# First layer of a two-layer network on 512 tokens at a time, behind a banded attention, on one core of Trainium2

## The chip, the core and the metric

The kernel runs on one core of one Trainium2 chip. Times are device microseconds (us) of an execution. The kernel before takes 738.41 us in the median of three runs (738.12 to 741.0).

## The reference, cut to what matters

```python
# q, k, v: batch 4, 8 heads, 768 positions, 64 per head; n_global = 8, n_local = 96
scores = q @ k.T / sqrt(64)
keep   = (key < n_global) | ((0 <= rel) & (rel < n_local))       # rel = query - key
scores = where(keep, scores - slope[head] * dist, -1e9)          # ALiBi distance
a      = softmax(scores)                                          # the sum gets 1e-9
x      = (a @ v) laid out as 3072 tokens x 512
h      = x @ w_in                                                 # 512 -> 2048
out    = (0.5 * h * (1 + erf(h / sqrt(2)))) @ w_out               # GELU, 2048 -> 512
```

w_in and w_out arrive as 64-bit numbers; all arithmetic is of 32-bit floats.

## The kernel before, in words

The 3072 tokens are cut into twelve **chunks** of 256 tokens, the 2048 hidden columns into eight **slices** of 256. A **step** t is one pair (chunk, slice) from the list `STEPS`; there are 96. The matmuls read their operands in a form that keeps fewer bits of a number, so every number that matters is split into a high part (ending in h) and a low part (ending in l), and each product is three matmuls: high times high, high times low, low times high.

In step t the first layer (`m1`, L463) fills one PSUM bank `h{t}`: two halves f of 128 hidden columns, for each of four pieces d of the 512 inputs three matmuls over 256 tokens. That is 24 matmuls of 128x256, each with its own 128x128 stationary weights (`winh`, `winl`), and the moving operand is x of the chunk (`xh`, `xl`). Then `gelu`: ScalarE (ACT) makes `gr` from `h` (L473), GpSimd (POOL) makes the high part `gh` (helper line L145), VectorE (DVE) the low part `gl` (helper line L151). The second layer (`m2`, L493) has `gh`/`gl` of 128 tokens as stationary operand, and 512 columns of `wouth`/`woutl` as moving operand: 12 matmuls of 128x512 that add into two accumulators `acc{c}_0`, `acc{c}_1`, one bank each, over all eight slices of the chunk. After the last slice ACT copies them out and a DMA stores them.

The attention of a chunk is spread over some ten steps, from `START[c]` on (`att`, the tables `EV` and `EVN` say at which step each part comes): k, q and v are loaded and split (POOL and DVE), scores `s` (PE, L338), masked on DVE (`n`, L343), the exponential on ACT (L358) in two batches of four heads, the division by the sum on POOL (`n<-n,su`, L371), transposes `t` (PE, L384), their copy in two parts `pt` (ACT L391, then DVE L151), `av` (PE, L426), and from that `t1`, `t3` (ACT, DVE) and the two parts of x. Every `s`, `t` and `av` takes a PSUM bank from its first matmul to the end of its last reader. Chunks 0 and 1 (`NATIVE`) use another form. While steps 0 to 8 run, the weights are still being loaded and split (`split_weights`, ACT and DVE), one slice after another; therefore chunks 0 and 1 go through slices 2 to 7 side by side, and chunks 2 to 11 one after another.

PSUM has eight banks. Two belong to the pool `ps_acc` (accumulators), six to the pool `ps` (`h`, `s`, `t`, `av`, and the accumulators of chunk 1).

The code is written step by step: `run` emits for each T the first layer of step T+1, the attention parts that fall on T, and the second layer of step T. The framework's scheduler then sets the order on each engine by priorities, its own estimate of times and the buffers that are free, and chooses the bank of each tile. Each engine works in its order; a matmul waits for what it reads, and the first one into a bank for the last reader of the bank's previous tile.

Of the kernel before, what the change touches and what calls it, by code (L numbers as in the profile page):

```python
# [68 lines left out]
class Fast:  # L69
    def __init__(self, tc, ctx, qT, kT, v, w, out, limits):  # L70
        self.tc, self.nc = tc, tc.nc
        self.qT, self.kT, self.v, self.w, self.out = qT, kT, v, w, out
# [322 lines left out]
    def av_mm(self, c, h):  # L395
        nc = self.nc
        p, hh = divmod(h, 2)
        pts = self.parts(c)
        first = c % CPB == 0
        pt = self.pt_t.pop((c, h))  # L400
        vt = self.vt.pop((c, h))
        if h == 0:
            self.x[c] = (self.xp.tile([P, NP, CT], F32R, name=f"xh{c}", tag="xh"),
                         self.xp.tile([P, NP, CT], F32R, name=f"xl{c}", tag="xl"))
        if c in NATIVE:
            if hh == 0:
                self.avp = self.bank([P, 2, 2, D], f"av{c}_{p}", [P, 2, 2, 2 * D])
            av = self.avp
            for i, (j, a) in enumerate(pts):
                vi = (a if first else 2 * j + a)  # L410
                js = [x for x in pts if x[0] == j]
                nc.tensor.matmul(av[:, hh, j, :], lhsT=pt[:, i, :], rhs=vt[:, vi, :],
                                 start=(j, a) == js[0], stop=(j, a) == js[-1])
            if hh == 1:
# [4 lines left out]
                self.xs[c, p] = xs
            return  # L420
        av = self.bank([P, 2, 2, P], f"av{c}_{h}")
        for i, (j, a) in enumerate(pts):
            vi = (a if first else 2 * j + a)
            js = [x for x in pts if x[0] == j]
            start, stop = (j, a) == js[0], (j, a) == js[-1]
            nc.tensor.matmul(av[:, j], lhsT=vt[:, vi], rhs=pt[:, i], start=start, stop=stop)  # L426
        if hh == 0:
            self.t3[c, p] = (self.sm.tile([P, 2, P], F32, name=f"t1_{c}_{p}", tag="t1", bufs=1),
                             self.sm.tile([P, 2, P], F32, name=f"t3_{c}_{p}", tag="t3", bufs=1))
        t1, t3 = self.t3[c, p]  # L430
# [4 lines left out]
        nc.vector.tensor_tensor(out=t3[hr], in0=av[hr, :, 0, :], in1=t1[hr], op=ALU.add)
        if hh == 1:
            xh, xl = self.x[c]
            t3f = t3.rearrange("p j q -> p (j q)")
# [10 lines left out]
        nc.scalar.copy(xh, xt)  # L449
        self.lo_dve(xl, xt, xh)  # L450

    def m1(self, t, f):
        nc = self.nc
        c, s = STEPS[t]
        xh, xl = self.x[c]
        wh, wl = self.win[s]
        if f == 0:
            self.h[t] = self.bank([P, 2, CT], f"h{t}")
        hp = self.h[t]
        n = 0  # L460
        for d in range(NP):
            for w, x in ((wh, xh), (wh, xl), (wl, xh)):
                nc.tensor.matmul(hp[:, f, :], lhsT=w[:, d, f * P:(f + 1) * P], rhs=x[:, d, :],  # L463
                                 start=n == 0, stop=n == 3 * NP - 1)
                n += 1

    def gelu(self, t):
        nc = self.nc
        hp = self.h.pop(t)
        gh = self.gp.tile([P, 2, CT], F32R, name=f"gh{t}", tag="gh")  # L470
        gl = self.gp.tile([P, 2, CT], F32R, name=f"gl{t}", tag="gl")
        gr = self.gp.tile([P, 2, CT], F32, name=f"gr{t}", tag="gr", bufs=1)
        self.table(nc.scalar.activation(out=gr, in_=hp, func=AF.Gelu))  # L473
# [4 lines left out]
    def m2(self, t, k):
        nc = self.nc
        c, s = STEPS[t]  # L480
        gh, gl = self.g[t]
        wh, wl = self.wout[s]
        if s == 0:
            if c == 1:
                self.acc[c, k] = self.bank([P, DM], f"acc{c}_{k}")
            else:
                self.acc[c, k] = self.ps_acc.tile([P, DM], F32, name=f"acc{c}_{k}", tag="ps_acc")
        acc = self.acc[c, k]
        ks = slice(k * P, (k + 1) * P)
        n = 0  # L490
        for f in range(2):
            for g, w in ((gh, wh), (gh, wl), (gl, wh)):
                nc.tensor.matmul(acc, lhsT=g[:, f, ks], rhs=w[:, f, :],  # L493
                                 start=s == 0 and n == 0, stop=s == NST - 1 and n == 5)
                n += 1
        if s == NST - 1:
# [284 lines left out]
```

## Time and profile before

| | |
|---|---|
| median of three runs | 738.41 us |
| the profiled execution: time, span of its profile | 739.55 us, 737.5 us |
| granted TensorE clock, mean | 0.998 |
| TensorE matmul busy (PE) | 715.7 us, 97% of the span |
| VectorE busy (DVE) | 504.1 us, 68% |
| ScalarE busy (ACT) | 355.2 us, 42 activation table loads among it |
| GpSimd busy (POOL) | 309.7 us, 42% |
| first-layer matmuls, 128x256 | 2304 |
| second-layer matmuls, 128x512 | 1152 |

Busy PE time is the time in which at least one matmul is in flight. A matmul's row is longer than the distance to the next one, since matmuls overlap: what one costs in a row of its kind is the distance from start to start, and that is read from the chain of the work that ended last, or from the timeline. "Idle before" is the time that an engine stood still ahead of an instruction, with what ended it.

### The profile page before, as it was taken

What the parts mean: (1) busy time and instruction counts of PE and PEld (TensorE: products, weight loads), DVE (VectorE), ACT (ScalarE), POOL (GpSimd) and SP (SyncE); (2) the same over time, 40 slices, a digit from 0 to 9 for tenths busy, and PEclk for the clock granted to TensorE, in tenths of its full rate; (3) what the DMA queues carried; (4) which work ended last, traced back from release to release, by engine and by line L of the source; (5) the groups of instructions that cost most, each with busy time, mean ns of one, the idle gap of its engine ahead of it and who ended that gap; (6) DMA issues with size and microseconds to landing.
All of it is one profiled execution on the core that took longest, in us unless ns stands there. A gap on an engine that the chain in (4) does not pass through costs nothing.

```text
span 737.5 us, 13431 instructions
## 1 busy us (share of the span) xinstructions
PE 715.7 (97%) x4617; PEld 647.1 (88%) x4617; DVE 504.1 (68%) x1317; ACT 355.2 (48%) x906; POOL 309.7 (42%) x572
## 2 busy tenths in 40 slices
PE   5999999898999999999999999999999999999996
PEld 3778999788999999999889999999899999989995
DVE  6998898956857867856757867857758767634210
ACT  4666656355355455355355355354455455452101
POOL 2311125665345555553544654643544654431110
PEclk9999999999999999999999999999999999999999
DMA  8986524225424434334335434234335331100000
GB/s 244 275 218 221 160 89 144 74 62 157 118 85 126 132 100 116 101 92 128 107 97 135 116 108 129 87 101 133 101 104 137 111 112 44 44 16 1 30 1 32
DMA packets 74395, 80.91 MB, mean 110 GB/s; under 512 B 12368, under 2 KB 63056, under 8 KB 74320
## 3 DMA queue, kind: packets, MB, share of 16 engines
q1 hardware_dynamic: 70144, 73.16, 34.9%
q10 hardware_dynamic: 4176, 6.82, 2.6%
q8 instruction: 38, 0.62, 0.3%
q14 instruction: 37, 0.30, 0.1%
HBM read 73.66 MB, written 6.29 MB: 108 GB/s over the span
## 4 chain that ended last, share of the span: by engine, by line
PE 71%; DVE 10%; DMA 7%; POOL 5%; ACT 4%; issue 3%; SPq 1%; ACTq 0%; DVEq 0%; POOLq 0%
PE acc L493 29%; PE h L463 29%; PE av L426 4%; PE s L338 4%; PE t L384 4%; POOL n L371 3%; DMA w<-w 3%; DMA vr<-v 2%; DMA c<-w 2%; ACT n L358 2%; DVE wb L188 1%; DVE wb L186 1%; DVE n L343 1%; POOL gh L145 1%; DVE wb L184 1%
## 5 line engine op out<-in xcount | busy, mean ns | idle before, releaser
L463 PE MATMUL h<-xh,winh 128*128 128x256 f32 x768 | 219.7, 286 | 0.0
L463 PE MATMUL h<-xl,winh 128*128 128x256 f32 x768 | 218.5, 285 | 0.0
L463 PE MATMUL h<-xh,winl 128*128 128x256 f32 x768 | 217.1, 283 | 0.0
L493 PE MATMUL acc<-wouth,gh 128*128 128x512 f32 x384 | 153.7, 400 | 3.3 <-POOL gh L145 3.3
L493 PE MATMUL acc<-woutl,gh 128*128 128x512 f32 x384 | 151.1, 394 | 0.0
L463 PEld LDWEIGHTS h<-xh,winh 128*128 128x128 f32 x768 | 146.7, 191 | 2.3
L463 PEld LDWEIGHTS h<-xl,winh 128*128 128x128 f32 x768 | 146.9, 191 | 2.0
L463 PEld LDWEIGHTS h<-xh,winl 128*128 128x128 f32 x768 | 146.8, 191 | 0.4
L493 PE MATMUL acc<-wouth,gl 128*128 128x512 f32 x384 | 142.7, 395 | 1.2 <-DVE gl L151 1.2
L151 DVE TENSOR_TENSOR gl<-gr,gh 128x512 fp32r<-128x512 f32 x96 | 68.7, 716 | 91.2 <-POOL gh L145 91.2
L473 ACT ACTIVATE gr<-h 128x512 f32<-128x512 f32 x96 | 57.5, 599 | 147.1 <-PE h L463 102.4
L371 POOL TENSOR_SCALAR n<-n,su 128x256 f32<-128x256 f32 (+1 forms) x160 | 78.4, 511 | 83.6 <-DVE su L363 73.8
L145 POOL TENSOR_SCALAR gh<-gr 128x512 fp32r<-128x512 f32 x96 | 66.0, 687 | 99.6 <-ACT gr L473 99.6
L145 POOL TENSOR_SCALAR vt<-vr 128x256 fp32r<-128x256 f32 (+1 forms) x80 | 34.5, 432 | 150.1 <-DMA vr<-v 74.8
L358 ACT ACTIVATE n<-n,mn 128x256 f32<-128x256 f32 (+1 forms) x192 | 91.8, 480 | 4.9 <-DVE mn L343 4.4
L493 PEld LDWEIGHTS acc<-wouth,gl 128*128 128x128 f32 x384 | 72.1, 188 | 18.0 <-DVE gl L151 3.2
L493 PEld LDWEIGHTS acc<-wouth,gh 128*128 128x128 f32 x384 | 72.4, 189 | 15.8 <-POOL gh L145 5.0
L493 PEld LDWEIGHTS acc<-woutl,gh 128*128 128x128 f32 x384 | 72.5, 189 | 12.3
L391 ACT CAST pt<-t 128x512 fp32r<-128x512 f32 (+1 forms) x80 | 44.4, 555 | 67.8 <-PE t L384 60.3
L433 ACT COPY t<-av 64x256 f32<-64x256 f32 x80 | 29.4, 368 | 96.1 <-PE av L426 93.6
L343 DVE CUSTOM_DVE_ANT_0 n<-s,pen 128x256 f32<-128x256 f32 (+1 forms) x192 | 68.6, 392 | 4.4 <-PE s L338 2.8
L384 PE MATMUL t<-ident,n 128*128 128x128 f32 x352 | 60.5, 294 | 1.3 <-ACT gr L473 0.6
(87 smaller groups left out, 1071.4 us busy)
## 6 DMA issues: line engine op xcount, KB each, us to landing
w<-w SPq DMA_DIRECT2D x32, 512.0 KB, 4.1
c<-w SPq DMA_DIRECT2D x32, 512.0 KB, 3.8
kr<-kT SPq DMA_DIRECT2D x112, 112.0 KB, 2.7
qr<-qT SPq DMA_DIRECT2D x84, 128.0 KB, 2.9
vr<-v SPq DMA_DIRECT2D x48, 128.0 KB, 2.4
out<-o ACTq DMA_DIRECT2D x24, 256.0 KB, 2.2
kr<-kT SPq DMA_DIRECT2D x28, 128.0 KB, 2.7
vr<-v SPq DMA_DIRECT2D x32, 96.0 KB, 2.2
```

The costliest lines, as they stand in the source:

```text
L145: self.nc.gpsimd.tensor_scalar(out=out, in0=in_, scalar1=scale, scalar2=0.0, op0=ALU.mult, op1=ALU.add)
L151: self.nc.vector.tensor_tensor(out=out, in0=in_, in1=hi.bitcast(F32), op=ALU.subtract)
L338: nc.tensor.matmul(sp[:, j, :w], lhsT=qq[:, hh, j * P:(j + 1) * P], rhs=kt[:, t, 0 if first else j, :w], start=t == 0, stop=t == 1)
L343: nc.vector.tensor_tensor_reduce(out=nn[:, j, :w], in0=sp[:, j, :w], in1=pen, scale=-slope(h), scalar=3e38, op0=ALU.add, op1=ALU.min, accu ...
L358: ins = nc.scalar.activation(out=nn[:, j, :w], in_=nn[:, j, :w], func=AF.Exp, bias=mn[:, i:i + 1], scale=-1.0, accum_out=su[:, i:i + 1])
L371: nc.gpsimd.tensor_scalar(out=nn[:, j, :w], in0=nn[:, j, :w], scalar1=su[:, i:i + 1], scalar2=0.0, op0=ALU.mult, op1=ALU.add)
L384: nc.tensor.transpose(tp[:, i, :], nn[:, j, a * P:(a + 1) * P], self.ident)
L391: nc.scalar.copy(pt[:, :, 0, :], tp[:, :n, :])
L426: nc.tensor.matmul(av[:, j], lhsT=vt[:, vi], rhs=pt[:, i], start=start, stop=stop)
L463: nc.tensor.matmul(hp[:, f, :], lhsT=w[:, d, f * P:(f + 1) * P], rhs=x[:, d, :], start=n == 0, stop=n == 3 * NP - 1)
L473: self.table(nc.scalar.activation(out=gr, in_=hp, func=AF.Gelu))
L493: nc.tensor.matmul(acc, lhsT=g[:, f, ks], rhs=w[:, f, :], start=s == 0 and n == 0, stop=s == NST - 1 and n == 5)
```

## The change

Four things change together.

- **Pairs.** From slice 2 on chunks 0 and 1 share each step, chunks 2 and 3 stay alone, and from chunk 4 on the chunks rotate: chunk 4 does slices 0 to 3 alone (steps 32 to 35), then chunks 4 and 5 share slices 4 to 7 (steps 36 to 43), chunks 5 and 6 slices 0 to 3 (steps 44 to 51), chunks 6 and 7 slices 4 to 7, and so on; chunk 11 does its last four slices alone (steps 92 to 95). A shared step is one half f of a slice for two chunks: `m1` has 12 matmuls of 128x512 in place of 24 of 128x256, with 12 weight loads in place of 24. There are 68 shared steps and 28 others, 96 as before. `m2` keeps 12 matmuls of 128x512 in each step; in a shared step they go into four accumulators, three into each.
- **The ring.** x of three chunks lies in one tile for each part (`xall`), chunk c at place c mod 3, so that two chunks can be one moving operand: two runs of 256 tokens, side by side or with the third place between them.
- **One pool.** The eight banks are one pool. In the rotation four of them hold accumulators all the time, so four are left for `h`, `s`, `t` and `av`, where six were.
- **The attention's starts.** Chunk 4 starts its attention at step 18 (before 19), chunk 5 at 24 (27), chunks 6 to 11 four steps earlier than before; the first matmul of chunk c is now in step 8c - 4 (chunk 5 on), before in step 8c.

```diff
-START = [-10, -6, 4] + [8 * c - 13 for c in range(3, NCH)]
-
-STEPS = [(0, 0), (0, 1), (1, 0), (1, 1)] + [(c, s) for s in range(2, NST) for c in range(2)]
-STEPS += [(c, s) for c in range(2, NCH) for s in range(NST)]
+START = [-10, -6, 4, 11, 18, 24] + [8 * c - 17 for c in range(6, NCH)]
+STEPS += [((0, 1), s, f) for s in range(2, NST) for f in range(2)]
...
-        self.xp = pool("xp", 3)
+        self.xp = pool("xp")
...
-        self.ps_acc = pool("ps_acc", 2, space=PSUM)
-        self.ps = pool("ps", 6, space=PSUM)
+        self.ps = pool("ps", 8, space=PSUM)
+        self.xall = tuple(self.xp.tile([P, NP, 3, CT], F32R, name=n) for n in ("xh", "xl"))
...
+    def tokens(self, x, cs, d):
+        i = sorted(c % 3 for c in cs)
+        return x[:, d, i[0], :] if len(i) == 1 else x[:, d, i[0]:i[1] + 1:i[1] - i[0], :]
...
+        if len(cs) == 1:
+            out, f, ds = self.h[t][:, half * CT:(half + 1) * CT], half, range(NP)
+        else:
+            out, ds = self.h[t].rearrange("p (k q) -> p k q", k=2), range(2 * half, 2 * half + 2)
+        for d in ds:
+            for n, (w, x) in enumerate(((wh, xh), (wh, xl), (wl, xh))):
+                nc.tensor.matmul(out, lhsT=w[:, d, f * P:(f + 1) * P], rhs=self.tokens(x, cs, d),
+                                 start=d == 0 and n == 0, stop=d == NP - 1 and n == 2)
...
+    def m2(self, t, half):
+        cs, s, f = STEPS[t]
+        if len(cs) == 1:
+            self.m2_block(t, cs[0], half, [(half * P, 0), (CT + half * P, 1)])
+            return
+        c = cs[half]
+        at = CT * sorted(x % 3 for x in cs).index(c % 3)
+        for k in range(2):
+            self.m2_block(t, c, k, [(at + k * P, f)])
```

What this does to the order shows at three places. In the rows a name's first number is the step (`h49`, `gh49`) or the chunk and the head (`t7_6`) or the chunk and its half (`acc5_0`); the last number only tells tiles apart.

**PE in step 49**, the last matmuls of `h49` and what follows. Before:

```order
L463 MATMUL h49_5217<-xh6_4406,winl1_539 128x256
L338 MATMUL s7_6_5256<-k7_6_5162,q7_3_5161 128x256 x4
L384 MATMUL t7_3_5264<-ident_112,n7_3_4911 128x128 x4
L493 MATMUL acc6_0_5272<-wouth0_400,gh48_5108 128x512
L493 MATMUL acc6_0_5272<-woutl0_401,gh48_5108 128x512
L493 MATMUL acc6_0_5272<-wouth0_400,gl48_5109 128x512
L493 MATMUL acc6_0_5272<-wouth0_400,gh48_5108 128x512
L493 MATMUL acc6_0_5272<-woutl0_401,gh48_5108 128x512
L493 MATMUL acc6_0_5272<-wouth0_400,gl48_5109 128x512
L493 MATMUL acc6_1_5297<-wouth0_400,gh48_5108 128x512
L493 MATMUL acc6_1_5297<-woutl0_401,gh48_5108 128x512
L493 MATMUL acc6_1_5297<-wouth0_400,gl48_5109 128x512
```

After:

```order
L479 MATMUL h49_5087<-xh_98,winl2_674 128x512
L394 MATMUL t7_6_5094<-ident_111,n7_6_4790 128x128 x4
L348 MATMUL s8_2_5114<-k8_2_5045,q8_1_5044 128x256 x4
L394 MATMUL t7_7_5122<-ident_111,n7_7_4822 128x128 x4
L514 MATMUL acc5_0_4184<-wouth2_675,gh49_5108 128x512
L514 MATMUL acc5_0_4184<-woutl2_676,gh49_5108 128x512
L514 MATMUL acc5_1_4188<-wouth2_675,gh49_5108 128x512
L514 MATMUL acc5_1_4188<-woutl2_676,gh49_5108 128x512
```

Before, `gh49` is first read seventeen rows behind the first one shown, after the whole second layer of step 48, two attention heads' scores and one `av`. Now the second layer of step 48 lies ahead of `h49`, and only two transposes of four matmuls and one head's scores stand between the last `h49` matmul and the first reader of `gh49`; `t7_7` takes the bank that `h49` leaves.

**PE in step 21** (chunk 2 alone, the attention of chunks 3 and 4 beside it). Before:

```order
L463 MATMUL h21_2629<-xh2_1527,winl5_1076 128x256
L338 MATMUL s4_2_2667<-k4_2_2588,q4_1_2587 128x256 x4
L384 MATMUL t3_7_2675<-ident_112,n3_7_2334 128x128 x3
L493 MATMUL acc2_0_2317<-wouth4_928,gl20_2532 128x512
L493 MATMUL acc2_0_2317<-wouth4_928,gh20_2531 128x512
L493 MATMUL acc2_0_2317<-woutl4_929,gh20_2531 128x512
L493 MATMUL acc2_0_2317<-wouth4_928,gl20_2532 128x512
L493 MATMUL acc2_1_2341<-wouth4_928,gl20_2532 128x512
L493 MATMUL acc2_1_2341<-wouth4_928,gh20_2531 128x512
L493 MATMUL acc2_1_2341<-woutl4_929,gh20_2531 128x512
L493 MATMUL acc2_1_2341<-wouth4_928,gl20_2532 128x512
L426 MATMUL av3_6_2688<-pt3_6_2646,vt3_3_0_2577 128x256 x3
```

After:

```order
L479 MATMUL h21_2492<-xh_98,winl5_1059 128x256
L394 MATMUL t3_7_2530<-ident_111,n3_7_2181 128x128 x3
L435 MATMUL av3_6_2543<-pt3_6_2509,vt3_3_0_2463 128x256 x3
L514 MATMUL acc2_0_2164<-wouth5_1060,gh21_2524 128x512
L514 MATMUL acc2_0_2164<-woutl5_1061,gh21_2524 128x512
L514 MATMUL acc2_1_2188<-wouth5_1060,gh21_2524 128x512
L514 MATMUL acc2_1_2188<-woutl5_1061,gh21_2524 128x512
L514 MATMUL acc2_0_2164<-wouth5_1060,gl21_2525 128x512
```

Before, the first reader of `gh21` comes after the second layer of step 20 and two heads' scores; now three transposes and three `av` matmuls lie between.

**POOL around step 47**, where a batch of four heads is divided by its sums. Before:

```order
L145 TENSOR_SCALAR gh46_4958<-gr46_4960 128x512
L371 TENSOR_SCALAR n7_0_4753<-n7_0_4753,su7_0_4751 128x256 x2
L371 TENSOR_SCALAR n7_1_4783<-n7_1_4783,su7_0_4751 128x256 x2
L371 TENSOR_SCALAR n7_2_4881<-n7_2_4881,su7_0_4751 128x256 x2
L371 TENSOR_SCALAR n7_3_4911<-n7_3_4911,su7_0_4751 128x256 x2
L145 TENSOR_SCALAR gh47_5024<-gr47_5026 128x512
L145 TENSOR_SCALAR k7_6_5162<-kr7_3_5051 128x2x224
L145 TENSOR_SCALAR gh48_5108<-gr48_5110 128x512
```

After:

```order
L155 TENSOR_SCALAR xh_98<-t3_7_1_4817 128x256
L155 TENSOR_SCALAR gh46_4860<-gr46_4862 128x512
L155 TENSOR_SCALAR gh47_4914<-gr47_4916 128x512
L381 TENSOR_SCALAR n7_4_4664<-n7_4_4664,su7_1_4662 128x256 x2
L381 TENSOR_SCALAR n7_5_4702<-n7_5_4702,su7_1_4662 128x256 x2
L381 TENSOR_SCALAR n7_6_4790<-n7_6_4790,su7_1_4662 128x256 x2
L381 TENSOR_SCALAR n7_7_4822<-n7_7_4822,su7_1_4662 128x256 x2
L155 TENSOR_SCALAR gh48_4986<-gr48_4988 128x512
```

Before, `gh47` stands behind the eight divisions; now ahead of them. It is the same in steps 59, 63 and 71; in steps 51, 55, 67, 75 and 79 `gh` still stands behind the eight.

More of the change, by code (lines that the diff above doesn't have):

```diff
@@ L31 @@
 NATIVE = (0, 1)
-START = [-10, -6, 4] + [8 * c - 13 for c in range(3, NCH)]
-STEPS = [(0, 0), (0, 1), (1, 0), (1, 1)] + [(c, s) for s in range(2, NST) for c in range(2)]
-STEPS += [(c, s) for c in range(2, NCH) for s in range(NST)]
+START = [-10, -6, 4, 11, 18, 24] + [8 * c - 17 for c in range(6, NCH)]
+PAIRED = 4
+STEPS = [((0,), 0, None), ((0,), 1, None), ((1,), 0, None), ((1,), 1, None)]
+STEPS += [((0, 1), s, f) for s in range(2, NST) for f in range(2)]
+STEPS += [((c,), s, None) for c in range(2, PAIRED) for s in range(NST)]
+STEPS += [((PAIRED,), s, None) for s in range(4)]
+for c in range(PAIRED, NCH - 1):
+    STEPS += [((c, c + 1), s, f) for s in range(4 if (c - PAIRED) % 2 == 0 else 0, 8 if (c - PAIRED) % 2 == 0 else 4)
+              for f in range(2)]
+STEPS += [((NCH - 1,), s, None) for s in (range(4, 8) if (NCH - 1 - PAIRED) % 2 == 0 else range(4))]
+FIRST = {c: min(t for t, x in enumerate(STEPS) if c in x[0]) for c in range(NCH)}
+LAST = {c: max(t for t, x in enumerate(STEPS) if c in x[0]) for c in range(NCH)}
 EV = {"split": (-1, 0, 3, 4), "v": (3, 4, 7, 8), "s": (0, 1, 4, 5), "exp": (2, 6),
@@ L402, in av_mm @@
         if h == 0:
-            self.x[c] = (self.xp.tile([P, NP, CT], F32R, name=f"xh{c}", tag="xh"),
-                         self.xp.tile([P, NP, CT], F32R, name=f"xl{c}", tag="xl"))
+            self.x[c] = tuple(x[:, :, c % 3, :] for x in self.xall)
         if c in NATIVE:
@@ L450, in turn, with m1 @@
         self.lo_dve(xl, xt, xh)
-    def m1(self, t, f):
+    def tokens(self, x, cs, d):
+        i = sorted(c % 3 for c in cs)
+        return x[:, d, i[0], :] if len(i) == 1 else x[:, d, i[0]:i[1] + 1:i[1] - i[0], :]
+    def m1(self, t, half):
         nc = self.nc
-        c, s = STEPS[t]
-        xh, xl = self.x[c]
+        cs, s, f = STEPS[t]
+        xh, xl = self.xall
         wh, wl = self.win[s]
[L457 to L465, printed above, removed]
+        if half == 0:
+            self.h[t] = self.bank([P, 512], f"h{t}")
+        if len(cs) == 1:
[6 more added lines that the diff above has]
+                                 start=d == 0 and n == 0, stop=d == NP - 1 and n == 2)
     def gelu(self, t):
@@ L469, in gelu @@
         hp = self.h.pop(t)
-        gh = self.gp.tile([P, 2, CT], F32R, name=f"gh{t}", tag="gh")
-        gl = self.gp.tile([P, 2, CT], F32R, name=f"gl{t}", tag="gl")
-        gr = self.gp.tile([P, 2, CT], F32, name=f"gr{t}", tag="gr", bufs=1)
+        gh = self.gp.tile([P, 512], F32R, name=f"gh{t}", tag="gh")
+        gl = self.gp.tile([P, 512], F32R, name=f"gl{t}", tag="gl")
+        gr = self.gp.tile([P, 512], F32, name=f"gr{t}", tag="gr", bufs=1)
         self.table(nc.scalar.activation(out=gr, in_=hp, func=AF.Gelu))
@@ L476, in gelu, with m2_block @@
         self.g[t] = (gh, gl)
-    def m2(self, t, k):
+    def m2(self, t, half):
+        cs, s, f = STEPS[t]
+        if len(cs) == 1:
[5 more added lines that the diff above has]
+            self.m2_block(t, c, k, [(at + k * P, f)])
+    def m2_block(self, t, c, k, parts):
         nc = self.nc
-        c, s = STEPS[t]
         gh, gl = self.g[t]
[L482 to L487, printed above, removed]
+        wh, wl = self.wout[STEPS[t][1]]
+        if t == FIRST[c]:
+            self.acc[c, k] = self.bank([P, DM], f"acc{c}_{k}")
         acc = self.acc[c, k]
-        ks = slice(k * P, (k + 1) * P)
         n = 0
-        for f in range(2):
+        for at, f in parts:
             for g, w in ((gh, wh), (gh, wl), (gl, wh)):
-                nc.tensor.matmul(acc, lhsT=g[:, f, ks], rhs=w[:, f, :],
-                                 start=s == 0 and n == 0, stop=s == NST - 1 and n == 5)
+                nc.tensor.matmul(acc, lhsT=g[:, at:at + P], rhs=w[:, f, :], start=t == FIRST[c] and n == 0,
+                                 stop=t == LAST[c] and n == 3 * len(parts) - 1)
                 n += 1
-        if s == NST - 1:
+        if t == LAST[c]:
             o = self.sm.tile([P, DM], F32, name=f"o{c}_{k}", tag="o")
```

## The prediction

> **What bounds the kernel now.** I read the windows of the span first, then PE's waits, then the chain that ended last for the price of one matmul, then the timeline at single places.
>
> Windows, with the busy time of each engine in each stretch:
>
> ```profile
> core 0: us, PE busy (x) PEld busy (x) DVE busy (x) ACT busy (x) POOL busy (x), PEclk, DMA share, GB/s
> 66.00:100.00 34.00, 33.20 (x217) 31.26 (x218) 28.87 (x55) 19.13 (x35) 4.36 (x5) 1.00 0.52 158
> 100.00:140.00 40.00, 38.70 (x254) 34.70 (x254) 36.58 (x79) 22.50 (x56) 21.15 (x28) 1.00 0.32 94
> 140.00:195.00 55.00, 51.62 (x350) 46.78 (x349) 37.46 (x104) 27.32 (x68) 30.41 (x60) 1.00 0.38 105
> 195.00:363.00 168.00, 167.55 (x1139) 154.42 (x1138) 120.60 (x320) 83.43 (x218) 83.66 (x158) 1.00 0.39 112
> 363.00:531.00 168.00, 167.26 (x1137) 153.90 (x1136) 120.98 (x321) 83.45 (x218) 81.82 (x157) 1.00 0.39 111
> 531.00:674.00 143.00, 142.34 (x966) 131.41 (x965) 94.36 (x246) 70.83 (x186) 64.79 (x119) 1.00 0.26 75
> 674.00:737.50 63.50, 57.52 (x362) 51.43 (x361) 9.39 (x20) 8.34 (x14) 6.63 (x11) 0.98 0.05 18
> ```
>
> From 195 us on PE is busy all the time; DVE is at 72%, ACT and POOL at 50%, the DMA engines at 39%. Between 100 and 195 us PE stands still for 4.7 us (1.30 + 3.38), with DVE at 91% in the first 40 of them: there the weights are still being made. PE's waits from 195 us to the end:
>
> ```profile
> engine line waited for: us in total, times, longest us
> PE acc L493 <- POOL gh L145: 1.8, 4, 0.7
> ```
>
> So 540 us hold 1.8 us of waiting (the last 6 us of the span are the last copy and its store). Each matmul saved there is time saved, and each new wait of PE is time lost. The price of a matmul, from runs of one kind in the chain that ended last:
>
> ```profile
> 198.53 0.35 PE av L426 x3
> 198.88 2.87 PE h L463 x24
> ...
> 206.46 2.75 PE acc L493 x12
> ...
> 212.40 0.48 PE s L338 x4
> 212.88 0.33 PE t L384 x3
> ```
>
> A 128x256 matmul of the first layer costs 2.87/24 = 119.6 ns, a 128x512 one 2.75/12 = 229.2 ns, a head's scores 0.48 us, three transposes 0.33, three `av` 0.35. Two of 256 cost 239.2 ns, one of 512 229.2: 10 ns less.
>
> [...]
>
> **The first layer (removed and added).** 68 shared steps, 24 matmuls each become 12: 68 x 12 = 816 pairs x 10.0 ns = 8.2 us less. 56 of these steps (6.7 us) lie in the rotation, where PE is the bound: counted in full. The other 12 (1.4 us) are steps 4 to 15, by the count of matmuls from about 92 to 180 us. Those up to 140 us lie where PE is nearly always busy, the later ones where it waits for the softmax, the banks and the weights anyway. Ends: all kept, all lost; I take half, -0.7 of the gain. That the 512 columns lie in two runs of 256 is shown by no row; the nearest is the second layer's 229.2 ns with one run, the other end two of 256, 239.2 ns. I take 229.2, since the number of columns and the contiguous output are the same.
>
> **What has to happen between the two layers.** The last first-layer matmul of a step, ACT, POOL and DVE, where nothing else is queued:
>
> ```profile
> 703.19 0.28 PE L463 MATMUL h<-xh,winl 128*128 128x256 f32 x1
> ...
> 703.51 0.60 ACT L473 ACTIVATE gr<-h 128x512 f32<-128x512 f32 x1 [5.02 <-PE h L463]
> ...
> 704.18 0.62 POOL L145 TENSOR_SCALAR gh<-gr 128x512 fp32r<-128x512 f32 x1 [5.00 <-ACT gr L473]
> ...
> 704.84 0.69 DVE L151 TENSOR_TENSOR gl<-gr,gh 128x512 fp32r<-128x512 f32 x1 [4.93 <-POOL gh L145]
> ```
>
> From the start of that matmul `gh` is there after 704.80 - 703.19 = 1.61 us, `gl` after 2.34 us. With other work queued it is longer; step 49 of before:
>
> ```profile
> 416.17 0.28 PE L463 MATMUL h<-xh,winl 128*128 128x256 f32 x1
> ...
> 416.49 0.60 ACT L473 ACTIVATE gr<-h 128x512 f32<-128x512 f32 x1 [0.85 <-PE h L463]
> ...
> 416.77 0.60 PE L384 MATMUL t<-ident,n 128*128 128x128 f32 x4
> ...
> 417.13 0.48 PE L493 MATMUL acc<-wouth,gh 128*128 128x512 f32 x1
> ...
> 417.46 0.41 POOL L145 TENSOR_SCALAR xh<-t 128x256 fp32r<-128x256 f32 x1
> ...
> 417.83 0.73 POOL L145 TENSOR_SCALAR k<-kr 128x448 fp32r<-128x448 f32 x1
> ...
> 418.53 0.61 POOL L145 TENSOR_SCALAR gh<-gr 128x512 fp32r<-128x512 f32 x1
> ...
> 420.92 0.40 PE L493 MATMUL acc<-wouth,gh 128*128 128x512 f32 x1
> ```
>
> Here `gh` took 419.14 - 416.17 = 2.97 us, because POOL did an `xh` and a `k` first, and PE asked for it only after 4.75 us.
>
> **Fewer banks (new wait in the rotation).** With four banks for `h`, `s`, `t`, `av` the order can no longer start the next `h` early. After the last matmul of `h49` there now stand two transposes of a head and one head's scores: 0.23 (that matmul) + 0.36 + 0.48 + 0.36 = 1.43 us until PE asks for `gh49` (0.36 for a head's transposes: 416.77 to 417.13). That is 0.2 us short of the free chain and 1.5 short of the one with POOL's queue. The same place comes once in eight steps: by the same count 2.2 us of work in step 41, 2.3 in 57, 1.3 in 65, 1.4 in 73. Waits: at least 0.2 to 0.4 each in three of them, at most 0.8, 1.5, 0.7, 1.7 and 1.5, together 0.8 to 6.2 us. POOL's queue ahead of `gh49` no longer has the `k`, only `xh`, so I stay near the lower end: 0.5 each, +2.5. What is queued behind such a wait on PE is one `av`, the scores and the next `h`; DVE, ACT and POOL use the time to catch up. The banks themselves: `t7_7` needs `h49`'s, free 0.32 + 0.60 = 0.92 us after the last matmul (703.19 to the end of `gr`), with 1.07 of work between; elsewhere in the rotation 2.8 us or more of matmuls lie between a bank's last matmul and its next tile. No wait counted; DVE late there is part of (b).
>
> **The attention of chunks 4 and 5 moved forward (steps 16 to 36).** Chunks 3 to 6 start 7, 6 and 7 steps apart, before 8: the attention of three chunks on 20 steps, before on 24, so DVE's 72% become some 80% (an estimate: its attention work by 24/20, `gl` as before). In step 21 the work between `h21` and `gh21` is 0.12 + 0.33 + 0.35 = 0.80 us against 1.61 to 2.97: a wait of 0.8 to 2.2; I take 1.3, as no `k` stands ahead on POOL. At the end of chunk 4 only one head's `av` lies between the last transpose and the `av` that needs it, 0.09 + 0.48 = 0.57 us, and `pt` between takes ACT and DVE:
>
> ```profile
> L151 DVE TENSOR_TENSOR pt<-t,pt 128x512 fp32r<-128x512 f32 x56 | 38.4, 686 | 6.2 <-ACT pt L391 5.4
> L391 ACT CAST pt<-t 128x512 fp32r<-128x512 f32 x56 | 32.9, 587 | 49.2 <-PE t L384 45.9 <-DVE vt L311 3.0
> ```
>
> That is 0.32 from the last matmul's start to ACT, as at 703.19, then 0.59 and 0.69, 1.6 us at least: a wait of 1.0, and 2.0 with two exponentials ahead on ACT; I take 1.1. Smaller shortfalls (step 30, the `pt` of chunk 5) 0 to 2, I take 0.6. Together +3.0, ends 1.8 and 6.2. The k, q and v of these chunks are loaded through SP up to four steps earlier, into buffers that chunks before leave as early; the cover is a DMA share of 0.39. Uncovered, a late `vr` would hold POOL's `vt`.
>
> **The divisions on POOL (less waiting).** Before, every fourth `gh` stands behind eight divisions; step 47:
>
> ```profile
> 403.80 3.84 POOL L371 TENSOR_SCALAR n<-n,su 128x256 f32<-128x256 f32 x8 [2.63 <-DVE su L363]
> 407.62 0.78 POOL L145 TENSOR_SCALAR gh<-gr 128x512 fp32r<-128x512 f32 x1
> ```
>
> At such places PE's 1.8 us of waiting arise. In four of these steps `gh` now goes first, 3.84 us earlier, and what is late next is the first `t`, which has eight second-layer matmuls, 1.8 us, ahead of it. Relief 0 to 1.8; I take 0.7.
>
> **No cost.** The ring: its writers wait for no matmul, as the tenant three chunks back has been read for eight steps. The tail: four more steps without attention, but there PE goes without a wait already (the 5.02 us that ACT idles at 703.51 are PE's work). Table loads: 42, as before.
>
> **Sum.** -8.2 + 0.7 + 2.5 + 3.0 - 0.7 = -2.7 us. Against the profiled execution 739.55 - 2.7 = 736.85; that execution lies 1.1 us over the median, and from the median it is 738.41 - 2.7 = **735.7 us**.
>
> **Rivals.** About 0.5% (3.7 us) is what a measurement of this kernel can tell from no change: 734.7 to 742.1.
> (a) The waits stay at their lower ends, 0.8 + 1.8, and the relief comes whole: -8.2 + 0.7 + 2.6 - 1.8 = -6.7, some 732 us. For it: POOL and ACT are half idle, and a wait at one place gives slack at the next. Against: DVE's queue.
> (b) Slower: POOL's queue stands ahead of `gh` at the places with four banks as it did in step 49 of before. All five rotation waits at the upper end, 6.2, and those of steps 16 to 36 with them, 6.2: -8.2 + 0.7 + 12.4 = +4.9, 743 us. It decides from 11.2 us of new waits on (8.2 - 0.7 + 3.7); against it, `xh` is the only thing that the order puts late ahead of `gh49`.
> (c) The 512 columns in two runs cost as much as two matmuls of 256, 239.2 ns: no gain, -0 + 2.5 + 3.0 - 0.7 = +4.8, 743 us. For it, no row shows such an operand; against, 256 and 512 columns in one run differ by a fixed 10 ns.
> (d) The 10 ns are only partly a price of the matmul; the rest goes with the columns (119.6 ns are 0.467 ns a column, 229.2 are 0.448) and stays in the wider one. [...]
>
> **How the numbers follow.** Forecast (waits eat about two thirds of the gain, within 0.5%) 0.40; (a) 0.40; (b) 0.10; (c) 0.06; (d) 0.04. Faster by over 0.5% 0.40, within 0.5% 0.40 + 0.04 = 0.44, slower 0.16. The range reaches down to the whole gain with the lower waits, -8.2 + 2.6 - 1.8 = -7.4, 731.0, and up to 741.6, which leaves out most of (b) and (c).
>
> **What would show it.** In the chain after, 12 first-layer matmuls in 2.75 us; were it 2.87, (c) holds. PE's waits from 195 us on: `acc` for `gh` some 4 us, `av` for `pt` 1 to 2, mostly before 350 us; 2 us in all would be (a), over 11 (b). POOL's divisions behind `gh` in steps 47, 59, 63, 71. The prediction is wrong if PE waits where I saw cover: for a bank's reader on DVE, or for k, q, v.

## The result, and the profile after

The changed kernel takes 770.56 us in the median of four runs (767.61 to 770.84), the one before 738.26 us on the same chip (738.08 to 741.0): a ratio of 1.042, 95% interval 1.038 to 1.046. Forecast were 735.7 us and a range up to 741.6. The profiled execution took 770.51 us, its span is 768.6 us.

The windows of the span, the same stretches as before (the last one now ends at 768.6):

```profile
core 0: us, PE busy (x) PEld busy (x) DVE busy (x) ACT busy (x) POOL busy (x), PEclk, DMA share, GB/s
66.00:100.00 34.00, 33.09 (x201) 30.23 (x202) 29.14 (x55) 19.40 (x37) 4.92 (x5) 1.00 0.52 163
100.00:140.00 40.00, 36.92 (x167) 30.43 (x166) 34.84 (x76) 21.43 (x53) 18.24 (x26) 0.91 0.28 85
140.00:195.00 55.00, 52.21 (x282) 43.27 (x282) 35.34 (x100) 25.62 (x62) 28.97 (x58) 1.00 0.28 80
195.00:363.00 168.00, 159.40 (x1026) 141.30 (x1025) 124.75 (x337) 83.64 (x223) 83.80 (x161) 0.99 0.41 116
363.00:531.00 168.00, 161.35 (x820) 133.87 (x818) 114.12 (x300) 81.80 (x215) 79.35 (x151) 1.00 0.37 106
531.00:674.00 143.00, 135.07 (x671) 113.22 (x672) 92.35 (x243) 68.13 (x182) 63.66 (x119) 0.98 0.29 84
674.00:768.60 94.60, 88.17 (x440) 74.02 (x438) 16.76 (x32) 14.66 (x26) 10.09 (x17) 0.98 0.05 18
```

PE was idle for 0.4, 0.7 and 0.7 us in the three long stretches from 195 to 674 us; now it is idle for 8.6, 6.7 and 7.9. DVE's share there is 74, 68 and 65%, close to before (72, 72 and 66%), so no engine has become full. And the granted clock, 1.00 in all of these stretches but the last before, is 0.91 in one and 0.99 and 0.98 in two others. PE's waits from 195 us on:

```profile
engine line waited for: us in total, times, longest us
PE acc L514 <- POOL gh L155: 14.6, 13, 2.9
PE av L435 <- DVE pt L161: 5.3, 7, 2.9
PE t L394 <- DVE mn L353: 1.2, 1, 1.2
```

The first two are the kinds of wait that the prediction named, at 20 us in place of 5 to 6. The first layer itself came out near its price; from the chain that ended last, shared steps:

```profile
449.87 2.75 PE h L479 x12
...
535.89 2.75 PE h L479 x12
...
593.13 2.79 PE h L479 x12
```

Where the time is lost shows best along the program. The table has the time at which the last first-layer matmul of a step starts, counted from the start of the span, less the same time in the kernel before, in us, each from one trace (the experiments are explained below):

| | step 7 | step 20 | step 36 | step 60 | step 84 | step 92 |
|---|---|---|---|---|---|---|
| after | -0.6 | 4.9 | 24.0 | 23.7 | 32.8 | 30.8 |
| before_new_starts | -1.7 | -0.6 | 21.0 | 21.4 | 21.2 | 17.1 |
| before_two_banks_held | -2.0 | -1.8 | -1.8 | 4.3 | 12.4 | 13.8 |
| gh_straight_from_act | -0.1 | -1.5 | 24.5 | 19.9 | 18.9 | 14.2 |
| later_rotation_half_divisions | -1.8 | 0.8 | 12.7 | 7.4 | 9.3 | 4.6 |

The column of step 36 holds some 4 to 5 us that are no loss: where the attention starts earlier, its PE work is done earlier, and the same kernels get it back between steps 84 and 92 (before_new_starts 21.2 to 17.1). After loses 5 us by step 20, some 15 between 20 and 36, and 11 in the rotation, where the gain of 6.7 us is already in.

Two places of the trace, for two things that can stand ahead of `gh` in POOL's queue. `vr` is a piece of v as it is loaded, `vt` its high part (POOL) and low part (DVE). Step 73, rows of SP, PE, ACT and POOL in order of time:

```profile
614.79 0.38 SPq L301 DMA_DIRECT2D vr<-v  x1
...
616.24 0.39 PE L479 MATMUL h<-xh,winl 128*128 128x512 f32 x1
...
616.67 0.60 ACT L488 ACTIVATE gr<-h 128x512 f32<-128x512 f32 x1 [2.43 <-PE h L479]
...
619.33 0.40 POOL L155 TENSOR_SCALAR vt<-vr 128x256 fp32r<-128x256 f32 x1 [3.26 <-DMA vr<-v]
619.70 0.40 POOL L155 TENSOR_SCALAR xh<-t 128x256 fp32r<-128x256 f32 x1
...
620.06 0.78 POOL L155 TENSOR_SCALAR gh<-gr 128x512 fp32r<-128x512 f32 x1
...
620.90 0.50 PE L514 MATMUL acc<-wouth,gh 128*128 128x512 f32 x1 [2.92 <-POOL gh L155]
```

`gr` was there at 617.27 and POOL idle, but `vt` stood ahead of `gh` in its queue and waited for the load of v, which SP had only begun to issue at 614.79, since there is one `vr` buffer. PE stood for 2.92 us. And the chain at step 55, whose `gh` stands behind the eight divisions (PE stood for 0.62 us):

```profile
487.85 4.01 POOL n L381 x8
491.86 0.60 POOL gh L155
492.50 3.06 PE acc L514 x12
```

### The profile page after: what moved, and what is told of

Its sections match the earlier page's. It is cut to its first block, busy times and chain, and to the rows that moved or that the text cites. A ratio compares the mean times of both kernels' runs of the same rounds, so it can differ in the third digit from the quotient of the medians.

```text
span 768.6 us, 11851 instructions
## 1 busy us (share of the span) xinstructions
PE 723.6 (94%) x3801; PEld 609.4 (79%) x3801; DVE 502.9 (65%) x1317; ACT 354.3 (46%) x906; POOL 305.2 (40%) x572
## 4 chain that ended last, share of the span: by engine, by line
PE 40%; POOL 5%; DVE 4%; DMA 4%; ACT 3%; issue 1%; SPq 0%; ACTq 0%; DVEq 0%; POOLq 0%
PE acc L514 19%; PE h L479 16%; POOL n L381 4%; DMA c<-w 3%; PE av L435 3%; PE s L348 2%; ACT n L368 1%; PE t L394 1%; POOL gh L155 1%; DVE k L161 1%; DVE wand L215 1%; DVE t L443 1%; DVE n L353 1%; ACT L368 1%; DVE pt L161 0%
## 5 line engine op out<-in xcount | busy, mean ns | idle before, releaser
L514 PE MATMUL acc<-wouth,gh 128*128 128x512 f32 x384 | 155.8, 406 | 19.0 <-POOL gh L155 18.6
L479 PE MATMUL h<-xh,winh 128*128 128x512 f32 (+1 forms) x496 | 172.3, 347 | 0.1
L479 PE MATMUL h<-xl,winh 128*128 128x512 f32 (+1 forms) x496 | 170.5, 344 | 0.3 <-DVE xl L161 0.3
L479 PE MATMUL h<-xh,winl 128*128 128x512 f32 (+1 forms) x496 | 170.5, 344 | 0.0
L514 PE MATMUL acc<-woutl,gh 128*128 128x512 f32 x384 | 153.4, 399 | 0.0
L161 DVE TENSOR_TENSOR gl<-gr,gh 128x512 fp32r<-128x512 f32 x96 | 73.5, 765 | 106.8 <-POOL gh L155 106.7
L514 PE MATMUL acc<-wouth,gl 128*128 128x512 f32 x384 | 130.5, 402 | 0.8 <-DVE gl L161 0.7
L479 PEld LDWEIGHTS h<-xh,winl 128*128 128x128 f32 x496 | 94.2, 190 | 11.4
L479 PEld LDWEIGHTS h<-xl,winh 128*128 128x128 f32 x496 | 94.4, 190 | 10.7 <-DVE xl L161 0.5
L479 PEld LDWEIGHTS h<-xh,winh 128*128 128x128 f32 x496 | 94.5, 190 | 10.5 <-issue 0.3
L514 PEld LDWEIGHTS acc<-wouth,gl 128*128 128x128 f32 x384 | 72.4, 192 | 17.1 <-DVE gl L161 2.4
L442 ACT COPY t<-av 64x256 f32<-64x256 f32 x80 | 29.3, 367 | 120.0 <-PE av L435 118.9
```

Of the source, the lines that this page charges most:

```text
L161: self.nc.vector.tensor_tensor(out=out, in0=in_, in1=hi.bitcast(F32), op=ALU.subtract)
L479: nc.tensor.matmul(out, lhsT=w[:, d, f * P:(f + 1) * P], rhs=self.tokens(x, cs, d), start=d == 0 and n == 0, stop=d == NP - 1 and n == 2)
L514: nc.tensor.matmul(acc, lhsT=g[:, at:at + P], rhs=w[:, f, :], start=t == FIRST[c] and n == 0, stop=t == LAST[c] and n == 3 * len(parts) - 1)
```

## The experiments

Times before are from runs of the kernel before on the same chip, 740.2 to 740.7 us in these groups.

**1. No shared step (solo_rotation).** Everything but the wide matmul:

```diff
-STEPS += [((0, 1), s, f) for s in range(2, NST) for f in range(2)]
+STEPS += [((c,), s, None) for s in range(2, NST) for c in range(2)]
...
-    STEPS += [((c, c + 1), s, f) for s in ... for f in range(2)]
+    STEPS += [((c + k,), s, None) for s in ... for k in range(2)]
```

> The changed kernel with every shared step undone into two steps of one chunk each: 128x256 matmuls as before, but the rotation, the ring, the one pool with four accumulators open, and the earlier starts of the attention stay. Theory (few banks and the earlier starts make PE wait for gh, pt and mn, and the waits of 3 us drop the clock): the loss stays although no wide matmul is left. The 5 us of steps 16 to 21 and the 10 us of steps 22 to 36 stay in full, of the rotation's 19 us perhaps half, and the 8 us of gain are gone: 755 to 775 us, PE waiting for POOL's gh 10 us or more. Rival (the wide matmul over two runs of 256 tokens brings the loss): back at 736 to 744 us.

768.24 us, ratio 1.036 (1.030 to 1.041). The rival is out: the loss is there without one matmul over two runs. The waits:

```profile
PE av L435 <- DVE pt L161: 11.9, 12, 3.1
PE acc L514 <- POOL gh L155: 7.8, 12, 1.6
```

`gh` is under the 10 us expected and `pt` twice what it is in after; the clock never halves behind the start (it is 1.00 in every stretch up to 690 us). So most of the loss, 28 us over the kernel before on its chip against 32, comes about without the clock. It also means that in the changed kernel itself the wide matmuls brought no time that can be measured: with them PE waits 10.8 us longer for `gh` and 6.0 less for `pt`, and 17.1 us run at half clock.

**2. Only chunks 0 and 1 share (pair_0_1_only).**

```diff
-START = [-10, -6, 4, 11, 18, 24] + [8 * c - 17 for c in range(6, NCH)]
+START = [-10, -6, 4] + [8 * c - 13 for c in range(3, NCH)]
...
...
-STEPS += [((c,), s, None) for c in range(2, PAIRED) for s in range(NST)]
...
+STEPS += [((c,), s, None) for c in range(2, NCH) for s in range(NST)]
```

> The changed kernel with only chunks 0 and 1 sharing steps; chunks 2 to 11 go one after another with 128x256 matmuls, the attention starts as before, and the ring and the one pool of eight banks stay (two accumulators open from step 16 on). Theory (four open accumulators and earlier starts): all loss behind step 16 goes; left are the early steps' 1.4 us of gain and up to 5.6 us of loss: 737 to 744 us, half-clock stretch only near the start. Rival (the ring or the one pool itself brings the loss): 755 us or more.

753.30 us, ratio 1.015 (1.010 to 1.020): neither. By step 24 it is 5.3 us late, the early loss expected, and it loses nothing from there to step 40, where after lost most. But it loses 3 us between steps 60 and 80 and 4 at step 88, where PE waits 2.7 us for DVE ahead of the matmul of the final flag, with 3.4 us at half clock behind it (from 701.6 us). Both lie where the code is that of before but for the pool and the ring; the order that came out is another one. Why it is worse there was not settled, so the ring and the one pool stay a possible cause of a few us.

**3. Two banks taken away (before_two_banks_held).** The kernel before:

```diff
+            if T == 36:
+                self.hold = [self.bank([P, 512], f"hold{k}") for k in range(2)]
+                for x in self.hold:
+                    self.nc.vector.memset(x[:, 0:1], 0.0)
...
+        for k, x in enumerate(self.hold):
+            self.nc.vector.tensor_copy(self.nmax[:, k:k + 1], x[:, 0:1])
```

> The kernel before, with two of its banks held by tiles that nobody uses from step 36 to the end, so that two accumulators, two idle tiles and four banks are there as in the rotation; two one-column VectorE copies at the end read them. Theory (four banks make the order put the reader of gh close behind h; POOL's queue does the rest): four places (steps 45, 53, 69, 77) now have 1.0 to 1.2 us of PE work between h and gh, so that gh costs 1 to 3 us there and some more behind the divisions: 746 to 758 us, all of the loss behind step 36. Rival (the number of banks does not matter, it is the wide steps' bursts or the earlier starts): 737 to 741 us.

753.95 us, ratio 1.019 (1.014 to 1.023), all of it behind step 36 (the table). PE's waits for `gh` over the whole span, in the kernel before and in this one:

```profile
PE acc L493 <- POOL gh L145: 3.3, 6, 1.1
...
PE acc L493 <- POOL gh L145: 14.3, 16, 1.6
```

Four banks alone bring this, with the order of chunks, the matmuls and the starts of before, and with the clock at 1.00 from 100 to 690 us.

**4. gh without GpSimd (gh_straight_from_act).**

```diff
+        self.table(nc.scalar.activation(out=gh, in_=hp, func=AF.Gelu))
         self.table(nc.scalar.activation(out=gr, in_=hp, func=AF.Gelu))
-        self.hi_pool(gh, gr)
```

> The changed kernel, with gh made by ScalarE as a second GELU of h (gh first, then gr) and not by GpSimd: gh needs no place in POOL's queue and is there 0.9 us after the last h matmul. Theory (POOL's in-order queue is what PE waits for, and the waits of 3 us drop the clock): PE's waits for gh fall from 18.6 to under 7 us, no half-clock stretch behind step 36, 742 to 755 us. Rival (the queue is not the matter: banks and the readers on VectorE and ScalarE hold PE anyway, waits only change their name): 762 us or more.

750.68 us, ratio 1.012 (1.006 to 1.017). By the table nothing is lost by step 20, and from 36 to 92 it goes 10.3 us faster than before, 4 to 5 of them the attention done ahead, the rest about the gain of the wide matmuls. From step 20 to 36 it loses 26 us, 7 more than after, and two half-clock stretches lie there (one in after). The waits:

```profile
PE av L435 <- DVE pt L161: 9.2, 9, 3.5
...
PE acc L514 <- DVE gl L161: 5.1, 7, 1.5
PE acc L514 <- ACT gh L488: 2.4, 8, 0.4
```

So the early and the rotation's loss lay in the way of `gh` through GpSimd; the loss of steps 20 to 36 is another, and it grew here. ScalarE has 0.6 us more to do in each step of this kernel; that this is why was not tested.

**5. The starts alone (before_new_starts).** In the kernel before, `START` of after.

> The kernel before with nothing changed but the table of the attention's starts: chunk 4 at step 18, chunk 5 at 24, chunks 6 to 11 four steps earlier, as in the change. Its matmuls, pools and order of chunks stay. Theory (three chunks' attention in 20 steps in place of 24 makes PE wait for pt, n and gh in steps 20 to 36, whatever the first layer looks like): 12 to 18 us lost there, 750 to 758 us, and nothing more lost behind step 44. Rival (with six banks for h, s, t, av the denser attention is hidden; the loss of steps 20 to 36 is one of banks): 738 to 742 us.

758.74 us, ratio 1.025 (1.022 to 1.029), just over the theory's range and all between steps 20 and 36, where two stretches of 3.4 us run at half clock (from 227.5 and 275.3 us). With six banks, two accumulators and the old matmuls:

```profile
PE av L426 <- DVE pt L151: 10.3, 9, 3.1
...
PE acc L493 <- POOL gh L145: 5.0, 5, 1.5
```

**6. One number (one_start_earlier).** The kernel before, with chunk 4 starting at step 18 in place of 19.

> The kernel before with one number changed: chunk 4's attention starts at step 18 in place of 19, seven steps behind chunk 3's in place of eight; all other chunks as before. It asks what of the 18 us of before_new_starts hangs on that one step. Theory (the load of the attention repeats every four steps of a chunk; eight steps apart two chunks' heavy steps fall on each other's light ones, seven apart the exponentials of one fall on the transposes and av of the other): 5 to 8 us lost by step 28, 742 to 748 us. Rival (only the density over all three chunks counts; one step of one chunk is lost in VectorE's slack of a quarter): 738 to 741.5 us.

747.32 us, ratio 1.010 (1.008 to 1.012). The trace is of the fastest of its six executions, 743.79 us. It is 5.6 us late at step 24 and 2.8 at step 36. The place is step 21:

```profile
218.78 0.55 SPq L291 DMA_DIRECT2D vr<-v  x1
...
220.79 0.48 ACT L391 CAST pt<-t 128x384 fp32r<-128x384 f32 x1 [1.38 <-PE t L384]
...
222.05 0.41 POOL L145 TENSOR_SCALAR vt<-vr 128x256 fp32r<-128x256 f32 x1 [2.16 <-DMA vr<-v]
222.49 0.43 DVE L311 TENSOR_TENSOR vt<-vr,vt 128x256 fp32r<-128x256 f32 x1 [1.54 <-POOL vt L145]
...
224.10 0.62 DVE L151 TENSOR_TENSOR xl<-t,xh 128x256 fp32r<-128x256 f32 x1
224.64 0.55 DVE L151 TENSOR_TENSOR pt<-t,pt 128x384 fp32r<-128x384 f32 x1
...
225.24 1.01 PE L426 MATMUL av<-pt,vt 128*128 128x256 f32 x3 [2.72 <-DVE pt L151]
```

ACT's part of `pt` is done at 221.27. DVE stands 1.54 us for `vt`, which POOL can't make before the load is there, and then does an add, two masks of chunk 4's scores and an `xl` ahead of `pt`. In the kernel before the same place has its `pt` 0.9 us after that `vt` starts, not 2.15 us, since chunk 4's masks come behind it:

```profile
221.47 0.43 DVE L311 TENSOR_TENSOR vt<-vr,vt 128x256 fp32r<-128x256 f32 x1 [0.36 <-POOL vt L145]
221.93 0.43 DVE L435 TENSOR_TENSOR t<-av,t 64x256 f32<-64x256 f32 x1
222.38 0.56 DVE L151 TENSOR_TENSOR pt<-t,pt 128x384 fp32r<-128x384 f32 x1
```

That exponentials and `av` of two chunks now share steps, as the expectation says, is in the tables of starts; that this makes the loss is argued. Shown is the chain above, and half clock behind it from 224.86 us on, for 3.41 us. The same rows stand in the same order at step 21 of after (DVE's `vt` at 228.62, `pt` at 230.76), before_new_starts (223.99, 226.14) and solo_rotation (230.12, 232.26), where PE waited 2.9, 3.1 and 3.1 us. The other waits for `pt` of steps 20 to 36 were not followed back.

**7. Half of the divisions on ScalarE (half_divisions_on_act).**

```diff
+                if k >= 2:
+                    nc.scalar.mul(nn[:, j, :w], nn[:, j, :w], su[:, i:i + 1])
+                    continue
```

> The changed kernel with the division of two of each four heads on ScalarE instead of GpSimd: 3.84 us of divisions ahead of gh in GpSimd's queue become 1.9, ScalarE gets some 45 us more work. Theory (GpSimd's queue is what gh waits in): the waits for gh fall from 18.6 to 8 to 12 us, the half-clock stretches behind steps 73 and 79 go, 755 to 763 us. Rival (the queue on GpSimd is not the matter, VectorE and the banks are): 766 us or more.

762.89 us, ratio 1.029 (1.025 to 1.032). The waits for `gh` fall to 8.3 us; `pt` rises to 10.0 and `gl` to 5.9. At step 36 it is 29.3 us late, 5 more than after, and the rotation makes up for more than that (25.7 at step 92). Half-clock stretches go from four to three, with one still near step 73.

**8. v behind gh (v_behind_gh).**

```diff
...
-            self.hi_pool(vt[:, :, hh, :], src)
+            self.after(self.hi_pool(vt[:, :, hh, :], src).ins, self.last_gh.ins, "gh goes ahead of v")
...
-        self.hi_pool(gh, gr)
+        self.last_gh = self.hi_pool(gh, gr)
```

> The changed kernel with one order fixed: on GpSimd the high part of v (vt) goes behind the gh of the same step, so that no gh stands behind a vt that waits for its load. Theory in its plain form (a gh behind a waiting vt is the loss of the rotation): waits for gh under 10 us, 755 to 763 us. Rival (GpSimd's queue is short of slack, a vt that goes later holds VectorE's low part of v behind it, then pt, then av): 770 us or more, the waits move from gh to pt.

779.32 us, ratio 1.051 (1.047 to 1.055), 9 us more than after, or 6 with each set against the kernel before on its own chip. The plain theory is out:

```profile
PE acc L514 <- POOL gh L155: 19.5, 17, 2.3
PE av L435 <- DVE pt L161: 13.6, 11, 2.7
```

`vt` behind `gh` costs more than a waiting `vt` ahead of it: the waits for `pt`, which stands behind `vt` on DVE, rose from 5.9 to 13.6 us, and those for `gh` did not even fall.

**9 and 10. A version with the causes taken down, wide and narrow.** Half of the divisions on ScalarE, the rotation from chunk 6, starts seven steps apart (later_rotation_half_divisions); and the same with its 52 shared steps undone (later_rotation_narrow, the edit of 1).

```diff
-START = [-10, -6, 4, 11, 18, 24] + [8 * c - 17 for c in range(6, NCH)]
+START = [-10, -6, 4, 11, 18, 25, 32] + [8 * c - 17 for c in range(7, NCH)]
...
-PAIRED = 4
+PAIRED = 6
```

> As half_divisions_on_act, and the rotation begins at chunk 6 in place of 4 (52 shared steps), so that the four steps by which the attention has to run ahead are spread: starts 4, 11, 18, 25, 32, then 8c - 17. Theory (density of the attention costs 15 us in steps 20 to 36, GpSimd's queue the rest): density is now 7, 7, 7, 7 steps, a third to a half of that loss is left, 738 to 748 us. Rival (any start ahead of a spacing of 8 costs as much as a denser one, spread or not): 752 us or more.

> As later_rotation_half_divisions (745.71 us), but each of the 52 shared steps undone into two steps of one chunk: 128x256 matmuls, the same rotation, starts, pools and half of the divisions on ScalarE. It prices the wide matmul in a kernel whose PE hardly waits. Theory (10 ns for each pair of matmuls are real and come out as time once the waits are gone): 52 x 12 x 10 ns = 6.2 us more, 750 to 758 us. Rival (the price is an artefact of reading rows; the time does not follow it): 742 to 748 us.

Wide 745.71 us, ratio 1.006 (1.003 to 1.008); narrow 754.12 us, ratio 1.016 (1.013 to 1.020). Set against the kernel before on its own chip, the wide one is some 8 us faster (5 to 11 by the intervals), where the price of a row makes 6.2. The narrow one waits longer for `pt` too (9.8 us against 5.7), so the 8 us are not the matmuls' alone. The clock halves in neither behind the start (its means are 0.997 and 0.998). The wide one is still slower than the kernel before: of the 12.7 us by step 36 some 8 are lost for good. None of the kernels run beats the one before.

**11. The cure in the kernel before (before_gh_straight_from_act).** The edit of 4 in the kernel before.

> The kernel before with gh made by ScalarE as a second GELU of h, as in gh_straight_from_act. It tells whether that edit is a gain in itself or only cures what the change brought. Theory (before, gh is asked for late enough that GpSimd's queue is covered, so there is nothing to gain; ScalarE's 0.6 us more per step delays gr, gl and pt): 738 to 750 us. Rival (a faster gh is worth the same 20 us in any kernel of this kind): 725 us or less.

754.71 us, ratio 1.018 (1.015 to 1.021): the rival is out, and the theory's range was too low. `gl` is made from `gr`, which is the second GELU now, and PE's waits for it are 9.4 us where the kernel before has 1.2:

```profile
PE acc L493 <- DVE gl L151: 9.4, 11, 1.9
```

**12. The clock by itself (still_tail).** PE is made to stand in steps 89, 90, 92 and 94 of the kernel before.

```diff
+    def still(self, n):
+        nc = self.nc
+        bp = self.bank([P, 512], f"still{self.T}")
+        ins = nc.tensor.transpose(bp[:, 0:P], self.ident, self.ident).ins
+        self.order(ins)
+        z = self.sm.tile([P, 512], F32, name=f"z{self.T}", tag="o")
+        nc.vector.tensor_copy(z[:, 0:P], bp[:, 0:P])
+        for _ in range(n):
+            self.hi_pool(z[:, 0:P], z[:, 0:P])
+        ins = nc.tensor.transpose(bp[:, P:2 * P], z[:, 0:P], self.ident).ins
+        self.order(ins)
...
+            if T in (89, 90, 92, 94):
+                self.still({89: 4, 90: 8, 92: 11, 94: 16}[T])
```

> The kernel before with PE made to stand still four times in its last steps, where nothing but the two layers runs: a transpose, a chain of 4, 8, 11 and 16 small GpSimd operations on its result (the output is not touched), and a transpose of what they leave; all matmuls around are held in the order of the code. It leaves PE idle for about 1.7, 2.8, 3.7 and 5 us. Theory (a stop of PE of about 3 us halves the granted clock for some us behind it): clock 1.0 behind the first, 0.5 for 3 to 7 us behind the last two. Rival (the half-clock stretches of the changed kernel come from something else than the stop itself, as the load on the other engines): clock 1.0 behind all four.

One run of 767.26 us. The four stops came to 17.2 us, longer than meant (2.75, 3.42, 4.57 and 6.46), and the clock halved behind all four, so the short stop of the expectation is missing. Windows around the second one, cut where the clock changes:

```profile
702.05:705.45 3.40, 3.40 (x22) 3.07 (x22) 0.46 (x1) 0.60 (x1) 0.62 (x1) 1.00 0.00 0
705.45:708.86 3.41, 1.03 (x6) 0.57 (x4) 0.53 (x2) 0.00 (x0) 1.55 (x6) 1.00 0.00 0
708.86:712.28 3.42, 2.37 (x11) 2.37 (x12) 0.16 (x1) 0.00 (x0) 0.83 (x3) 0.50 0.00 0
712.28:715.70 3.42, 3.42 (x17) 3.35 (x16) 0.00 (x0) 0.16 (x1) 0.00 (x0) 0.50 0.00 0
715.70:719.10 3.40, 3.40 (x20) 2.94 (x19) 0.69 (x1) 0.44 (x1) 0.62 (x1) 1.00 0.00 0
```

PEclk, the third figure from the end, is 0.50 in the two windows behind the one in which PE was busy for 1.03 of 3.41 us, while the other engines did little (POOL 1.55 us, DVE 0.53). So the clock halved behind the stop itself, without a load on the other engines.

## Why the prediction was wrong, point by point

- **The first layer, -8.2: held as a price, not as time.** By the chain twelve wide matmuls take 2.65 to 2.81 us, twenty-four narrow ones 2.83 to 2.89, and the two runs of 9 and 10 differ by about as much as that makes. Rival (c) is out by the rows, and they leave little room for (d); that (d) would end within 0.5% of no change, as its chance is counted, no run shows. In the changed kernel the waits ate the gain (experiment 1).
- **Steps 16 to 36, +3.0 with an upper end of 6.2: this step failed most.** The starts alone cost 18 us (experiment 5), one chunk one step earlier 7 (experiment 6). The prediction took three places one by one, spread the denser attention over DVE as a mean of some 80%, and hid the loads of v behind "a DMA share of 0.39". DVE stayed at 73%; at step 21 what failed is the order of single instructions in two queues, and the other places are open. The sentence "Uncovered, a late `vr` would hold POOL's `vt`" named the chain, and priced it at nothing. Step 21 was put as a wait for `gh21` of 1.3 us; it was one of 2.9 us for `pt3_6`, and the place had been read from PE's order and POOL's queue, not DVE's.
- **The rotation, +2.5 with ends of 0.8 and 6.2: under-sized.** Its five places (steps 41, 49, 57, 65 and 73) waited 0, 1.6, 0, 0.7 and 2.9 us, 5.2 together: inside the ends, and twice what was taken. Step 73 waited 2.9 us where 1.7 was the upper end and 0.5 taken, since the `vt` ahead of `xh` had been left out of POOL's queue. The reason given for the lower end, that only `xh` stands late ahead of `gh49`, was wrong in the same way: in step 49 a `vt` stood there too. The four banks' whole price is larger, 13.8 us in experiment 3, and the next point is a part of it.
- **`gh` behind the divisions, a relief of 0.7: failed, with the wrong sign.** The steps 43, 51, 55, 67, 75 and 79 waited 1.7, 0.8, 0.6, 1.7, 0.4 and 1.9 us, 7.2 together. The divisions are about as long as before (3.7 to 4.0 us for eight, before 3.84), but less PE work lies ahead of the reader; the relief looked only at the steps that got better.
- **The early steps, half of 1.4 lost: failed.** They lost 5 us, mostly in one wait of 3.1 us for `gh8`, behind eight divisions that took 6.3 us, and the half clock behind it:

```profile
124.80 6.29 POOL L381 TENSOR_SCALAR n<-n,su 128x256 f32<-128x256 f32 x8 [4.73 <-DVE su L373]
...
131.74 0.80 PE L514 MATMUL acc<-wouth,gh 128*128 128x512 f32 x1 [3.06 <-POOL gh L155]
```

- **The clock: not priced at all.** It was 1.00 before, and the sum took that as given. After, 17.1 us from 100 us on run at half clock, at most half of that, 8.5 us, lost. It is not what the loss hangs on: solo_rotation lost 28 us without it.
- **Rival (b)** had the right mechanism and sign, at a chance of 0.10 and 743 us. It took both upper ends, and left out the divisions, the early steps and the clock; those of steps 16 to 36 were too low by far.
- **The last sign of being wrong came true:** PE waited where cover had been seen, for v, by way of `vt` in steps 21 and 73.

Together the parts nearly make the whole: 18.1 us of starts, 13.8 of banks and 5.5 of the early steps, less the gain of 6.7 in the rotation, are 30.7 of the 32.3 us. That takes them as independent, which no run shows.

## What to carry to other kernels

Where an engine is busy all the time, a change that saves its work can also take away the slack behind which other queues hide (here PE was busy for 97% of the span before, and its waits for `gh` went from 3.3 to 18.6 us): ask of every wait it brings closer what stands *ahead* of the producer in its own in-order queue, down to the load that the first of them waits for. Moving one stage by one step is not a change of a mean load but a new interleaving of two queues, and here one such step cost 7 us with VectorE, ScalarE and GpSimd at or under 74%. Spend banks or slack first where the wide instruction pays, and price it against what the cover was worth: 8 us of shorter matmuls did not pay for 14 us of banks and 18 us of starts.

## What the runs showed of the hardware

In these runs the clock halved behind a window of 3.41 us in which PE stood for about half of the time. In the ten traces of this case with several changes of the clock, these lie on a grid of 3.41 us (in after the half-clock stretches begin at 130.73, 233.13, 622.25 and 670.04 us, 30, 114 and 14 steps of it apart, and PE stood for 2.05, 1.80, 2.06 and 1.87 us in the window ahead of each); in the other four I took the grid from the one change at the end. I cut the traces on it, from 100 us on to 8 us before the end of the matmuls, and summed PE's stops in each window at full clock: of 2564 windows with under 1.7 us of stop none was followed by half clock, of 7 with 1.7 to 1.81 three were, and of 21 with more all 21 (ends of matmuls are modelled, so the edge may be sharper).

So it matters where a stop lies. A wait of 1.88 us in v_behind_gh fell into one window and halved the clock of the next, which costs up to 1.7 us more (half of 3.41, an estimate):

```profile
284.20:287.62 3.42, 1.54 (x14) 1.33 (x13) 3.29 (x11) 1.73 (x6) 0.41 (x1) 1.00 0.44 132
287.62:291.03 3.41, 3.29 (x14) 3.02 (x15) 2.19 (x10) 2.95 (x8) 0.00 (x0) 0.50 0.07 22
```

One of 3.08 us at step 21 of solo_rotation lay across an edge, 1.7 us on one side and 1.4 on the other, and the clock stayed:

```profile
228.03:231.44 3.41, 1.76 (x15) 1.52 (x14) 1.54 (x6) 2.40 (x4) 0.76 (x2) 1.00 0.61 152
231.44:234.86 3.42, 1.84 (x8) 1.32 (x9) 3.38 (x14) 3.40 (x13) 1.03 (x3) 1.00 0.73 191
```

The way back shows too: of the half-clock windows from 100 us on to the last matmul, the three in which PE stood for 1.0 us or more were followed by another one, the 24 in which it stood for under 0.6 by full clock.

ScalarE's second GELU in place of a copy on GpSimd took PE's waits for `gh` from 18.6 to 2.4 us in the changed kernel and from 3.3 to 0.2 us in the one before, and made the changed one 20 us faster and the one before 14 us slower.
